# Attention scores as 64-row products of single heads, in the two halves of the array

## The chip, the cores and the metric

The kernel runs on one core of a Trainium2 chip. The metric is the device time of one execution, in microseconds. Before the change three runs took 1011.3 (median), 1008.68 and 1012.3 us. Engines are called PE (TensorE matmul; PEld is its weight load), DVE (VectorE), ACT (ScalarE), POOL (GpSimd) and SP (SyncE, which issues the DMAs). PSUM is the memory into which TensorE writes; the kernel uses it in eight buffers of one bank each.

## The reference

Pooled attention over eight batches, then two large layers (called FFN here):

```python
B, H, S, D = q.shape                      # 8, 8, 576, 64
k_p = k.reshape(B, H, Sp, 8, D).mean(axis=3)      # Sp = 72
v_p = v.reshape(B, H, Sp, 8, D).mean(axis=3)
scores = scale * np.matmul(q, k_p.transpose(0, 1, 3, 2))
scores = scores - np.max(scores, axis=-1, keepdims=True)
attn = np.exp(scores)
attn = attn / (np.sum(attn, axis=-1, keepdims=True) + 1e-09)
out = np.matmul(attn, v_p)
x = out.transpose(0, 2, 1, 3).reshape(4608, 512)
h = x @ w_in                              # 512 x 2048
g = np.maximum(0.01 * h, h)
return g @ w_out                          # 2048 x 512
```

All is F32. The kernel splits each FFN operand into a high and a low F32R part and adds three products.

## The kernel before, in words

**FFN.** The 4608 rows of x go through in chunks of 512. For a chunk and one of 16 slices of the hidden layer, `m1` adds 12 products of 512 columns into `ph` (lines 651 to 653), ACT applies the activation in place (656) and writes the high part `gh` (659), DVE writes the remainder `gl` (660). `m2` then adds 12 products into four accumulators `acc0` to `acc3` (675 to 677); it works on the slice two `m1` earlier. Each of the two yields twice, so there is a beat after every six products.

**Attention.** It is made beside the FFN. A batch's 576 queries are cut into tiles of 128 queries and one of 64, and the tiles are grouped into pieces (`PIECES`). For one tile the steps are:

- `q` (`q_unit`): four transpositions of two heads each into `qT`, so that rows 0 to 63 of a pair hold the even head's dimensions and rows 64 to 127 the odd head's (369, copied by ACT in 371).
- `sa` (`s_unit`), once for each half g of the eight heads: two products over 128 rows. Their moving operand `kT[:, p]` has 144 columns: 72 for the even head, with zeros in rows 64 to 127, and 72 for the odd head, with zeros in rows 0 to 63. So one product gives two heads' scores (394). Both go into one PSUM buffer. DVE takes the negative maximum of the four heads (402) and ACT four exps with their sums (404).
- `sb` (`norm_unit`): DVE adds 1e-9 to the four sums and takes the reciprocal (415, 416), POOL multiplies the exps into `at` (418, 422). For batch 0's tiles 2 and 3 DVE does this.
- `pu` (`p_unit`): three transpositions of `at` (443), which ACT and DVE copy into `pT` (445 to 453).
- `au` (`av_unit`), for a whole piece and half g: two head pairs, each with four products into a buffer of its own (468 to 471), copied out by ACT (479) and DVE (480) as the chunk's x.

Once for a batch, `ku` transposes the pooled keys and fills `kT` (328 to 337); `vu` fills the values and makes `v_rem` with two pairs of 32-row products (357, 360). POOL pools later batches' keys and values (229, 235); for batch 0 DVE and POOL share that.

**What sets the order.** PE runs in the order of the program (`manual_schedule`). Batch 0 goes first by a list written by hand (`FIRST`, where c is a step of converting the weights), with eight PSUM buffers in turn. From the "/" on, only the two of tag `a` serve attention, again in turn: `bank()` gives the next one, and PE waits until its last reader is done. Later batches' steps are listed by `line_up` and placed at the beats evenly over each chunk: six products or a multiple of six stand between two steps. Batch 1 runs beside the first eight slices of chunk 0, batches 2 to 7 beside the later chunks. The other engines' instructions are put in order by a scheduler from its own estimate of times, and each engine then runs its own in that order.

Tile pools: `one` has one buffer for a tag, `two` two, `three` three, `four` four. The exps' tile `e` (four heads) comes from `two`, except where `WIDE` gives batch 0's tiles room in the weights' buffers.

Of the kernel before, what the change touches and what calls it, by code (L numbers as in the profile page):

```python
# [10 lines left out]
F32 = mybir.dt.float32  # L11
# [4 lines left out]
ALU = mybir.AluOpType  # L16
# [8 lines left out]
def tile_pooled_attention_ffn(  # L25
# [38 lines left out]
    ]  # L64
    FIRST = (
# [259 lines left out]
    def place_k(b, sums, rem):  # L325
        pk = bank(b, f"pk{b}")
        for p in range(NK):
            nc.tensor.transpose(pk[:, p, :], sums[:, p, :, :].rearrange("s i d -> s (i d)"), ident)
        nc.scalar.mul(kT[0:64, :, 0, 0:MAIN], pk[0:64, :, 0:64], KSCALE)
        nc.vector.tensor_scalar_mul(kT[64:128, :, 1, 0:MAIN], pk[64:128, :, 64:128], KSCALE)  # L330
# [5 lines left out]
        nc.scalar.mul(kT[0:64, :, 0, MAIN:], prv[0:64, :, 0, :], KSCALE)  # L336
        nc.vector.tensor_scalar_mul(kT[64:128, :, 1, MAIN:], prv[64:128, :, 1, :], KSCALE)

    def place_v(b, sums, rem):
        for i in range(2):  # L340
# [38 lines left out]
    def wide_at(b, t, nm):  # L379
        return b == 0 and (nm, t) in WIDE  # L380

    def wide(b, t, g, nm, shape):
        if (nm, t) not in wides:
            wides[nm, t] = spare(*WIDE[nm, t], [P, 2, *shape], F32, f"{nm}{b}_{t}")
        return wides[nm, t][:, g]

    def s_unit(b, t, g, qT):

        n = tiles[b][t][1]
        pss = bank(b, f"pss{b}_{t}_{g}")  # L390
        sc = pss.rearrange("a p x -> a (p x)")[:, : 4 * SP]
        for i in range(2):
            p = 2 * g + i
            nc.tensor.matmul(  # L394
                sc[:n, 2 * SP * i : 2 * SP * (i + 1)], qT[:, p, :n],
                kT[:, p, :, :].rearrange("d i s -> d (i s)"), start=True, stop=True,
            )
        scv = sc.rearrange("a (h s) -> a h s", s=SP)
        e = wide(b, t, g, "e", [4, SP]) if wide_at(b, t, "e") else two.tile([P, 4, SP], F32, tag="e", name=f"e{b}_{t}_{g}")
        red = four.tile([P, 2, 4], F32, tag="red", name=f"red{b}_{t}_{g}")  # L400
        mx, sm = red[:, 0, :], red[:, 1, :]
        nc.vector.tensor_reduce(out=mx[:n], in_=scv[:n], axis=AX.X, op=ALU.max, negate=True)  # L402
        for h in range(4):
            ins = nc.scalar.activation(  # L404
                e[:n, h, :], scv[:n, h, :], AF.Exp, bias=mx[:n, h : h + 1],
                accum_out=sm[:n, h : h + 1],
            )
        if b == 0:
            anchor["act"] = ins
        return e, sm  # L410

    def norm_unit(b, t, g, e, sm):
        n = tiles[b][t][1]
        eng = nc.vector if b == 0 and t in NORM_DVE else nc.gpsimd
        nc.vector.tensor_scalar_add(sm[:n], sm[:n], 1e-9)
        nc.vector.reciprocal(sm[:n], sm[:n])  # L416
        at = wide(b, t, g, "at", [3, P]) if wide_at(b, t, "at") else three.tile([P, 3, P], F32, tag="at", name=f"at{b}_{t}_{g}")
        eng.tensor_tensor(  # L418
            at[:n, 0:2, :].rearrange("a i (h s) -> a (i h) s", h=2), e[:n, :, 0:MAIN],
            sm[:n].unsqueeze(2).broadcast_to([n, 4, MAIN]), op=ALU.mult,  # L420
        )
# [82 lines left out]
    def attention(b):  # L504
# [36 lines left out]
                    q_of[every[after]] = load_q(*every[after])  # L541
            return f

        def sa(t, g):
            def f():
                st["e", t, g] = s_unit(b, t, g, st["qT", t])
            return f

        def sb(t, g):
            def f():  # L550
                st["at", t, g] = norm_unit(b, t, g, *st["e", t, g])
            return f

        def pu(t, g):
# [7 lines left out]
        def au(j, g):  # L562
            def f():
# [3 lines left out]
        return {  # L567
            "loads": loads1 if b else loads, "lk": lk, "lv": lv, "ku": ku, "vu": vu,
            **{f"q{t}": qu(t) for t in range(len(where))},
            **{f"{n}{t}{g}": u(t, g) for n, u in (("sa", sa), ("sb", sb), ("pu", pu))  # L570
               for t in range(len(where)) for g in range(2)},
            **{f"au{j}{g}": au(j, g) for j in range(len(PIECES[b])) for g in range(2)},
        }
# [1 line left out]
    def line_up(pieces):  # L575
# [9 lines left out]
        for n, (b, j, t) in enumerate(flat):  # L585
# [5 lines left out]
                    add(b, "ku")  # L591
                add(b, f"q{t}")
            if (b, t) not in fresh:
                add(b, f"sa{t}0")
            if not first:
                add(b, f"pu{t - 1}0")
            if (b, t) not in fresh:
                add(b, f"sb{t}0")
            if nxt:
                add(nxt[0], f"q{nxt[2]}")  # L600
            add(b, f"sa{t}1")
            if n == 0 and t == 0:
                add(b, "vu")
            if last:
                if not first:
                    add(b, f"pu{t}0")
                    add(b, f"sb{t}1")
                else:
                    add(b, f"sb{t}1")
                    if nxt and nxt[0] == b:  # L610
                        add(b, f"sa{nxt[2]}0")
                        fresh[nxt[0], nxt[2]] = 1
                    add(b, f"pu{t}0")
                if nxt and nxt[0] == b and (nxt[0], nxt[2]) not in fresh:
                    add(b, f"sa{nxt[2]}0")
                    fresh[nxt[0], nxt[2]] = 1
# [222 lines left out]
```

## Time and profile before

| | us |
|---|---|
| median of three runs | 1011.3 |
| the profiled execution | 1009.92 |
| its span, first to last instruction | 1008.1 |
| PE busy | 960.3 |
| ACT busy | 427.4 |
| DVE busy | 366.3 |
| POOL busy | 177.7 |
| mean granted clock of TensorE | 0.978 |

The profile is of one execution. A row of a timeline gives the start from the span's beginning, the length, the engine, the line, the operation, out<-in, the part of the array used (rows*columns, for PE and PEld), the shape, and how many instructions are merged into the row (x4). What stands in brackets is how long the engine had been idle and what released it. Matmuls are pipelined, so the length of one (0.39 us for 512 columns) is longer than the distance to the next (0.23 us); distances between starts tell what a product costs.

### The profile page before, as it was taken

The numbers are of one execution on the slowest core, as the hardware profiler recorded it, in microseconds if no ns is written. First come the engines' busy times: TensorE is split into PE (matmuls) and PEld (weight loads), VectorE is DVE, ScalarE is ACT, GpSimd is POOL, SyncE is SP. The second block draws the span as 40 slices with busy tenths as digits, with TensorE's granted clock in tenths as the row PEclk, the third lists the DMA queues.
The fourth block names the chain that finished last, engine by engine and source line by source line (L and its number), as shares of the span: only waits on it lengthen the run. The fifth ranks groups of instructions, "written<-read, shape, count | busy, mean of one in ns | idle before, by whom it ended". The sixth has DMA issues, their size and how long they took to land.

```text
span 1008.1 us, 12812 instructions
## 1 busy us (share of the span) xinstructions
PE 960.3 (95%) x4584; PEld 785.7 (78%) x4584; DVE 366.3 (36%) x890; ACT 427.4 (42%) x1386; POOL 177.7 (18%) x292
## 2 busy tenths in 40 slices
PE   4569999999999999999999999999999999999998
PEld 4457778888887878878888788888887788888886
DVE  5998639223333222232222323232322322231111
ACT  4778657234433333434343425333434334332221
POOL 3602200501036510141013301031100001000000
PEclk8689999999999999999999999999999999999999
DMA  9954311302034301130012202020200020001001
GB/s 241 279 172 133 101 46 44 112 23 69 1 107 115 91 8 44 32 92 12 20 44 58 58 11 63 3 61 1 63 11 11 1 63 1 1 1 42 1 1 42
DMA packets 65006, 57.44 MB, mean 57 GB/s; under 512 B 39856, under 2 KB 48048, under 8 KB 64944
## 3 DMA queue, kind: packets, MB, share of 16 engines
q1 hardware_dynamic: 64944, 56.64, 19.8%
q8 instruction: 36, 0.59, 0.2%
q14 instruction: 26, 0.21, 0.1%
HBM read 46.14 MB, written 10.49 MB: 56 GB/s over the span
## 4 chain that ended last, share of the span: by engine, by line
PE 89%; DVE 4%; ACT 3%; issue 1%; DMA 1%; SPq 0%; POOL 0%; DVEq 0%; ACTq 0%; POOLq 0%
PE ph L651 13%; PE acc L675 13%; PE ph L653 13%; PE ph L652 13%; PE acc L677 13%; PE acc L676 13%; PE pss L394 4%; PE pp L443 2%; PE pq L369 2%; ACT e L404 2%; PE pa L468 1%; PE pa L469 1%; PE pa L471 1%; PE pa L470 1%; DVE w_t L187 1%
## 5 line engine op out<-in xcount | busy, mean ns | idle before, releaser
L651 PE MATMUL ph<-xh,w 128*128 128x512 f32 x576 | 236.2, 410 | 0.0
L675 PE MATMUL acc<-w,gh 128*128 128x512 f32 x576 | 234.7, 408 | 0.0
L653 PE MATMUL ph<-xh,w 128*128 128x512 f32 x576 | 227.2, 394 | 0.0
L652 PE MATMUL ph<-xl,w 128*128 128x512 f32 x576 | 227.0, 394 | 0.0
L677 PE MATMUL acc<-w,gl 128*128 128x512 f32 x576 | 225.7, 392 | 0.0
L676 PE MATMUL acc<-w,gh 128*128 128x512 f32 x576 | 225.5, 392 | 0.0
L656 ACT ACTIVATE ph<-ph 128x512 f32<-128x512 f32 x144 | 84.2, 585 | 275.6 <-PE ph L653 275.4
L660 DVE TENSOR_TENSOR gl<-ph,gh 128x512 fp32r<-128x512 f32 x144 | 99.4, 691 | 264.9 <-ACT gh L659 264.0
L418 POOL TENSOR_TENSOR at<-e,red 128x256 f32<-128x256 f32 (+1 forms) x76 | 47.3, 622 | 561.8 <-DVE red L416 428.0
L404 ACT ACTIVATE e<-pss,red 128x72 f32<-128x72 f32 (+1 forms) x320 | 98.0, 321 | 108.8 <-DVE red L402 107.3
L653 PEld LDWEIGHTS ph<-xh,w 128*128 128x128 f32 x576 | 109.3, 190 | 24.4
L677 PEld LDWEIGHTS acc<-w,gl 128*128 128x128 f32 x576 | 108.4, 188 | 24.1
L651 PEld LDWEIGHTS ph<-xh,w 128*128 128x128 f32 x576 | 109.4, 190 | 22.2 <-issue 1.4
L675 PEld LDWEIGHTS acc<-w,gh 128*128 128x128 f32 x576 | 108.4, 188 | 21.9 <-issue 1.9
L652 PEld LDWEIGHTS ph<-xl,w 128*128 128x128 f32 x576 | 109.6, 190 | 19.4
L676 PEld LDWEIGHTS acc<-w,gh 128*128 128x128 f32 x576 | 108.6, 189 | 19.2
L659 ACT CAST gh<-ph 128x512 fp32r<-128x512 f32 x144 | 85.2, 592 | 3.1
L402 DVE TENSOR_REDUCE red<-pss 128x4 f32<-128x288 f32 (+1 forms) x80 | 36.1, 454 | 99.6 <-PE pss L394 98.5
L404 ACT ACTIVATION_READ_ACCUMULATOR e<-pss,red 128x1 f32 (+1 forms) x320 | 65.8, 206 | 0.0
L394 PEld LDWEIGHTS pss<-kT,qT 128*128 128x128 f32 (+1 forms) x320 | 49.4, 192 | 14.7 <-ACT qT L371 5.0
L394 PE MATMUL pss<-kT,qT 128*128 128x144 f32 (+1 forms) x320 | 55.9, 303 | 4.2 <-ACT qT L371 4.2
L449 DVE TENSOR_TENSOR pT_lo<-pp,pT_hi 128x256 fp32r<-128x256 f32 (+1 forms) x80 | 31.6, 395 | 69.5 <-ACT pT_rem L446 68.7
(90 smaller groups left out, 857.3 us busy)
## 6 DMA issues: line engine op xcount, KB each, us to landing
out_dram<-o SPq DMA_DIRECT2D x35, 256.0 KB, 2.1
q<-in_q_dram SPq DMA_DIRECT2D x32, 256.0 KB, 4.2
w_bits<-in_moe_w_in_dram SPq DMA_DIRECT2D x16, 512.0 KB, 3.6
w_bits<-in_moe_w_out_dram SPq DMA_DIRECT2D x16, 512.0 KB, 3.4
k0raw<-in_k_dram SPq DMA_DIRECT2D x16, 256.0 KB, 3.7
k1raw<-in_k_dram SPq DMA_DIRECT2D x16, 256.0 KB, 4.4
v0raw<-in_v_dram SPq DMA_DIRECT2D x16, 256.0 KB, 4.2
v1raw<-in_v_dram SPq DMA_DIRECT2D x16, 256.0 KB, 5.4
```

Source lines behind the costliest of these rows:

```text
L394: nc.tensor.matmul(sc[:n, 2 * SP * i : 2 * SP * (i + 1)], qT[:, p, :n], kT[:, p, :, :].rearrange("d i s -> d (i s)"), start=True, stop=True,)
L404: ins = nc.scalar.activation(e[:n, h, :], scv[:n, h, :], AF.Exp, bias=mx[:n, h : h + 1], accum_out=sm[:n, h : h + 1],)
L418: eng.tensor_tensor(at[:n, 0:2, :].rearrange("a i (h s) -> a (i h) s", h=2), e[:n, :, 0:MAIN], sm[:n].unsqueeze(2).broadcast_to([n, 4, MAI ...
L651: nc.tensor.matmul(ph, w[:, 0, ks], xh[kk], start=kk == 0, stop=False)
L652: nc.tensor.matmul(ph, w[:, 0, ks], xl[kk], start=False, stop=False)
L653: nc.tensor.matmul(ph, w[:, 1, ks], xh[kk], start=False, stop=kk == NK - 1)
L656: nc.scalar.activation(ph, ph, AF.Prelu, alpha=0.01)
L659: casts.append(nc.scalar.copy(gh, ph))
L660: nc.vector.tensor_tensor(gl, ph, gh.bitcast(F32), op=ALU.subtract)
L675: nc.tensor.matmul(a, gh[:, r], hi, start=first, stop=False)
L676: nc.tensor.matmul(a, gh[:, r], lo, start=False, stop=False)
L677: nc.tensor.matmul(a, gl[:, r], hi, start=False, stop=last)
```

## The change

The scores of one tile are made in one step, `sa{t}`, in place of two. For each of the four head pairs there are two products of 64 rows and 72 columns: the even head's from rows 0 to 63 of `qT` and `kT`, the odd head's from rows 64 to 127. The even heads' scores go into one PSUM buffer and the odd heads' into another, so a step takes both buffers of tag `a`. `kT` no longer has zeros and loses a dimension; its clearing on POOL is gone. DVE takes a maximum for each of the two sides, ACT four exps for each. The tile `e` now holds all eight heads and comes from the pool with one buffer. The addition of 1e-9 and the reciprocal are made once for eight sums, and they stand at the end of `s_unit` and not in `norm_unit`. The lists `FIRST` and `line_up` name the one step where they named two, and a few neighbours change places.

The core of the diff:

```diff
-    kT = const.tile([P, NK, 2, SP], F32, name="kT")
+    kT = const.tile([P, NK, SP], F32, name="kT")
-    nc.gpsimd.memset(kT, 0.0)
...
-    def s_unit(b, t, g, qT):
+    def s_unit(b, t, qT):
         n = tiles[b][t][1]
-        pss = bank(b, f"pss{b}_{t}_{g}")
-        sc = pss.rearrange("a p x -> a (p x)")[:, : 4 * SP]
+        sides = [bank(b, f"pss{b}_{t}_{i}").rearrange("a p x -> a (p x)")[:, : 4 * SP] for i in range(2)]
+        for p in range(NK):
+            for i in range(2):
+                r = slice(64 * i, 64 * i + 64)
+                nc.tensor.matmul(
+                    sides[i][:n, SP * p : SP * (p + 1)], qT[r, p, :n], kT[r, p, :], start=True, stop=True
+                )
+        if wide_at(b, t, "e"):
+            e = wide(b, t, 0, "e", [4, SP], whole=True)
+        else:
+            e = one.tile([P, 2, 4, SP], F32, tag="e", name=f"e{b}_{t}")
+        ev = e.rearrange("a g (p i) s -> a i (g p) s", i=2)
+        red = four.tile([P, 2, 2, 4], F32, tag="red", name=f"red{b}_{t}")
+        mx, sm = (red[:, w].rearrange("a g (p i) -> a i (g p)", i=2) for w in range(2))
         for i in range(2):
-            p = 2 * g + i
-            nc.tensor.matmul(
-                sc[:n, 2 * SP * i : 2 * SP * (i + 1)], qT[:, p, :n],
-                kT[:, p, :, :].rearrange("d i s -> d (i s)"), start=True, stop=True,
-            )
...
+            scv = sides[i].rearrange("a (h s) -> a h s", s=SP)
+            nc.vector.tensor_reduce(out=mx[:n, i], in_=scv[:n], axis=AX.X, op=ALU.max, negate=True)
+            for p in range(NK):
+                ins = nc.scalar.activation(
+                    ev[:n, i, p, :], scv[:n, p, :], AF.Exp, bias=mx[:n, i, p : p + 1],
+                    accum_out=sm[:n, i, p : p + 1],
+                )
...
+        nc.vector.tensor_scalar_add(red[:n, 1], red[:n, 1], 1e-9)
+        nc.vector.reciprocal(red[:n, 1], red[:n, 1])
+        return e, red[:, 1]
...
     def norm_unit(b, t, g, e, sm):
-        nc.vector.tensor_scalar_add(sm[:n], sm[:n], 1e-9)
-        nc.vector.reciprocal(sm[:n], sm[:n])
+        e, sm = e[:, g], sm[:, g]
...
             if (b, t) not in fresh:
-                add(b, f"sa{t}0")
+                add(b, f"sa{t}")
+            if n == 0 and t == 0:
+                add(b, "vu")
...
-            add(b, f"sa{t}1")
-            if n == 0 and t == 0:
-                add(b, "vu")
```

The list by hand, before and after, up to the first value step:

```diff
-        "lk ku q0 q1 sa00 sb00 sa01 sb01 lv sa10 sb10 sa11 sb11 q2 sa20 sa21 vu pu00 pu10 c c q3 "
+        "lk ku q0 q1 sa0 sb00 sb01 lv sa1 sb10 sb11 q2 sa2 vu pu00 pu10 c c q3 "
```

Three places where the order of instructions moves follow. A row has the line, the operation, out<-in and the shape; `pss` are scores, `pa` value products, `pp` transposed probabilities, `ph` and `acc` the FFN's.

The first is PE's queue in batch 2, tile 2. Before:

```order
L394 MATMUL pss_2_0_2397<-kT,qT_2_2284 128x144 x2
L675 MATMUL acc_0_2258<-w_10_1497,gh_10_2236 128x512
L676 MATMUL acc_0_2258<-w_10_1497,gh_10_2236 128x512
L677 MATMUL acc_0_2258<-w_10_1497,gl_10_2237 128x512
L675 MATMUL acc_1_2262<-w_10_1497,gh_10_2236 128x512
L676 MATMUL acc_1_2262<-w_10_1497,gh_10_2236 128x512
L677 MATMUL acc_1_2262<-w_10_1497,gl_10_2237 128x512
L468 MATMUL pa_0_0_2413<-pT_hi,v_hi 128x256
```

After, from the last pair of the eight score products on:

```order
L397 MATMUL pss_2_0_2388<-kT,qT_2_2298 128x72
L397 MATMUL pss_2_1_2389<-kT,qT_2_2298 128x72
L653 MATMUL ph_12_2381<-xh_2_405,w_12_1594 128x512
L654 MATMUL ph_12_2381<-xl_2_409,w_12_1594 128x512
L655 MATMUL ph_12_2381<-xh_2_405,w_12_1594 128x512
L653 MATMUL ph_12_2381<-xh_3_406,w_12_1594 128x512
L654 MATMUL ph_12_2381<-xl_3_410,w_12_1594 128x512
L655 MATMUL ph_12_2381<-xh_3_406,w_12_1594 128x512
L476 MATMUL pa_0_0_2423<-pT_hi,v_hi 128x256
```

Six products stand between the scores and the value products in both; before, the scores held one of the two buffers there, now both (`pss_2_0` and `pss_2_1`).

The second is PE's queue in batch 1, tile 3. Before:

```order
L677 MATMUL acc_1_811<-w_3_620,gl_3_906 128x512
L394 MATMUL pss_3_0_1134<-kT,qT_3_1098 128x144 x2
L443 MATMUL pp_2_0_1144<-ident,at_2_0_1039 128x128 x3
L675 MATMUL acc_2_840<-w_3_620,gh_3_905 128x512
L676 MATMUL acc_2_840<-w_3_620,gh_3_905 128x512
```

After:

```order
L397 MATMUL pss_3_0_1136<-kT,qT_3_1112 128x72
L397 MATMUL pss_3_1_1137<-kT,qT_3_1112 128x72
L451 MATMUL pp_2_0_1160<-ident,at_2_0_1053 128x128 x3
L677 MATMUL acc_2_844<-w_3_622,gh_3_913 128x512
L678 MATMUL acc_2_844<-w_3_622,gh_3_913 128x512
```

The transposition follows its scores directly in both; before, it took the buffer that the scores did not hold.

The third is DVE's queue at the start, in batch 0, where `v1raw` and `vremraw` are the pooling of the values, which needs their DMA. Before:

```order
L337 TENSOR_SCALAR kT<-pkr_202 64x4x8
L402 TENSOR_REDUCE red_0_0_224<-pss_0_0_220 128x4
L229 TENSOR_TENSOR v1raw_139<-v1raw_139 128x2x256
L402 TENSOR_REDUCE red_0_1_239<-pss_0_1_235 128x4
L229 TENSOR_TENSOR vremraw_142<-vremraw_142 64x256
```

After:

```order
L337 TENSOR_SCALAR kT<-pkr_201 64x4x8
L229 TENSOR_TENSOR v1raw_138<-v1raw_138 128x2x256
L229 TENSOR_TENSOR vremraw_141<-vremraw_141 64x256
L229 TENSOR_TENSOR v1raw_138<-v1raw_138 128x2x128
L229 TENSOR_TENSOR vremraw_141<-vremraw_141 64x128
L235 TENSOR_TENSOR vsum_121<-v1raw_138 128x128
L409 TENSOR_REDUCE red_0_230<-pss_0_0_219 128x4
```

The first maximum of the scores moved behind five instructions of the values' pooling.

More of the change, by code (lines that the diff above doesn't have):

```diff
@@ L328, in place_k @@
             nc.tensor.transpose(pk[:, p, :], sums[:, p, :, :].rearrange("s i d -> s (i d)"), ident)
-        nc.scalar.mul(kT[0:64, :, 0, 0:MAIN], pk[0:64, :, 0:64], KSCALE)
-        nc.vector.tensor_scalar_mul(kT[64:128, :, 1, 0:MAIN], pk[64:128, :, 64:128], KSCALE)
+        nc.scalar.mul(kT[0:64, :, 0:MAIN], pk[0:64, :, 0:64], KSCALE)
+        nc.vector.tensor_scalar_mul(kT[64:128, :, 0:MAIN], pk[64:128, :, 64:128], KSCALE)
         pr = bank(b, f"pkr{b}")
@@ L335, in place_k @@
         prv = pr[:, 0, 0:64].rearrange("d (p i j) -> d p i j", p=NK, i=2)
-        nc.scalar.mul(kT[0:64, :, 0, MAIN:], prv[0:64, :, 0, :], KSCALE)
-        nc.vector.tensor_scalar_mul(kT[64:128, :, 1, MAIN:], prv[64:128, :, 1, :], KSCALE)
+        nc.scalar.mul(kT[0:64, :, MAIN:], prv[0:64, :, 0, :], KSCALE)
+        nc.vector.tensor_scalar_mul(kT[64:128, :, MAIN:], prv[64:128, :, 1, :], KSCALE)
     def place_v(b, sums, rem):
@@ L380, in wide_at, with wide @@
         return b == 0 and (nm, t) in WIDE
-    def wide(b, t, g, nm, shape):
+    def wide(b, t, g, nm, shape, whole=False):
         if (nm, t) not in wides:
             wides[nm, t] = spare(*WIDE[nm, t], [P, 2, *shape], F32, f"{nm}{b}_{t}")
-        return wides[nm, t][:, g]
-    def s_unit(b, t, g, qT):
+        return wides[nm, t] if whole else wides[nm, t][:, g]
+    def s_unit(b, t, qT):
         n = tiles[b][t][1]
-        pss = bank(b, f"pss{b}_{t}_{g}")
-        sc = pss.rearrange("a p x -> a (p x)")[:, : 4 * SP]
-        for i in range(2):
-            p = 2 * g + i
-            nc.tensor.matmul(
-                sc[:n, 2 * SP * i : 2 * SP * (i + 1)], qT[:, p, :n],
-                kT[:, p, :, :].rearrange("d i s -> d (i s)"), start=True, stop=True,
-            )
[L398 to L407, printed above, removed]
@@ L408, in s_unit @@
         if b == 0:
             anchor["act"] = ins
-        return e, sm
+        nc.vector.tensor_scalar_add(red[:n, 1], red[:n, 1], 1e-9)
+        nc.vector.reciprocal(red[:n, 1], red[:n, 1])
+        return e, red[:, 1]
     def norm_unit(b, t, g, e, sm):
@@ L542, in qu, with sa @@
             return f
-        def sa(t, g):
+        def sa(t):
             def f():
-                st["e", t, g] = s_unit(b, t, g, st["qT", t])
+                st["e", t] = s_unit(b, t, st["qT", t])
             return f
@@ L550, in f @@
             def f():
-                st["at", t, g] = norm_unit(b, t, g, *st["e", t, g])
+                st["at", t, g] = norm_unit(b, t, g, *st["e", t])
             return f
@@ L569, in attention @@
             **{f"q{t}": qu(t) for t in range(len(where))},
-            **{f"{n}{t}{g}": u(t, g) for n, u in (("sa", sa), ("sb", sb), ("pu", pu))
+            **{f"sa{t}": sa(t) for t in range(len(where))},
+            **{f"{n}{t}{g}": u(t, g) for n, u in (("sb", sb), ("pu", pu))
                for t in range(len(where)) for g in range(2)},
@@ L600, in line_up @@
                 add(nxt[0], f"q{nxt[2]}")
-            add(b, f"sa{t}1")
-            if n == 0 and t == 0:
-                add(b, "vu")
+            if last and not first:
+                add(b, f"pu{t}0")
+            add(b, f"sb{t}1")
             if last:
-                if not first:
+                if nxt and nxt[0] == b:
+                    add(b, f"sa{nxt[2]}")
+                    fresh[nxt[0], nxt[2]] = 1
+                if first:
                     add(b, f"pu{t}0")
[L607 to L616, printed above, removed]
                 if nxt and nxt[0] != b:
@@ L627, in line_up @@
                     add(nxt[0], "vu")
-            else:
-                add(b, f"sb{t}1")
         return out
```

4 rows, old and new, of the table FIRST are left out of this document.

## The prediction

> **What bounds the kernel now.** I read the page first: its span, busy times and the chain that ended last.
>
> ```profile
> span 1008.1 us, 12812 instructions
> PE 960.3 (95%) x4584; PEld 785.7 (78%) x4584; DVE 366.3 (36%) x890; ACT 427.4 (42%) x1386; POOL 177.7 (18%) x292
> PE 89%; DVE 4%; ACT 3%; issue 1%; DMA 1%; SPq 0%; POOL 0%; DVEq 0%; ACTq 0%; POOLq 0%
> ```
>
> TensorE carries 89% of the chain. The busy table by stage shows where that holds.
>
> ```profile
> 63.00:100.00 37.00, 32.02 (x153) 25.80 (x154) 31.81 (x75) 29.77 (x92) 5.89 (x10) 0.91 0.48 146
> 330.00:430.00 100.00, 100.00 (x483) 81.73 (x482) 29.18 (x74) 40.60 (x145) 21.11 (x35) 1.00 0.17 45
> ```
>
> The columns are PE, PEld, DVE, ACT, POOL, granted clock, DMA. Between 330 and 430 us PE is never idle, while ACT and DVE are busy 41 and 29 of 100 us: a microsecond added to or taken from TensorE's queue there goes into the time as it stands. Between 63 and 100 us PE already idles 5.0 of 37 us, so extra PE time there is partly absorbed. So I price the change by what a scores step costs in PE's queue, and by the waits that it puts there.
>
> **The step today.** The timeline of PE around one step (start, length, line; x4 because each F32 product runs as two passes):
>
> ```profile
> 603.09 0.39 PE L676 MATMUL acc<-w,gh 128*128 128x512 f32 x1
> 603.32 0.39 PE L677 MATMUL acc<-w,gl 128*128 128x512 f32 x1
> 603.54 0.65 PE L394 MATMUL pss<-kT,qT 128*128 128x144 f32 x4
> 603.94 0.49 PE L651 MATMUL ph<-xh,w 128*128 128x512 f32 x1
> 604.26 0.40 PE L652 MATMUL ph<-xl,w 128*128 128x512 f32 x1
> ```
>
> FFN products (FFN: the two big layers) start 0.23 us apart. From the last before the step to the second behind it is 0.94 us; less two intervals, the step costs 0.48 us, 0.12 for each pass of 144 columns, so 0.06 for 72. A full tile has two such steps: 0.96 us.
>
> Steps that use only 64 rows or 64 columns of the array exist already: a transposition of a 64-query tile (64*128), and that tile's scores (128*64).
>
> ```profile
> 287.24 0.39 PE L653 MATMUL ph<-xh,w 128*128 128x512 f32 x1
> 287.56 0.46 PE L369 MATMUL pq<-ident,q 64*128 64x64 f32 x4
> 287.95 0.50 PE L675 MATMUL acc<-w,gh 128*128 128x512 f32 x1
> 288.29 0.39 PE L676 MATMUL acc<-w,gh 128*128 128x512 f32 x1
> ...
> 293.82 0.39 PE L653 MATMUL ph<-xh,w 128*128 128x512 f32 x1
> 294.14 0.70 PE L394 MATMUL pss<-kT,qT 128*64 128x144 f32 x4
> 294.78 0.50 PE L675 MATMUL acc<-w,gh 128*128 128x512 f32 x1
> 295.12 0.40 PE L676 MATMUL acc<-w,gh 128*128 128x512 f32 x1
> ```
>
> By the same sum the first costs 1.05 − 0.46 = 0.59 us and the second 1.30 − 0.46 = 0.84. Their four passes account for 4 × 0.06 = 0.24 and 4 × 0.12 = 0.48. Both pay about 0.35 us more: going into another shape and back, the array runs empty (0.32 instead of 0.23 to the first product) and weight loads lie open. With the step's own first load (about 0.06 here) taken out, the toll is 0.30 us.
>
> What a weight load costs, and whether two parts of the array load at once, the v remainder's products show (32 rows each; the four belong to two different row groups). PEld rows:
>
> ```profile
> 324.19 0.29 PEld L357 LDWEIGHTS pv<-vremparts,spread 32*128 32x128 f32 x2 [0.35 <-DVE gl L660]
> ...
> 557.27 0.30 PEld L357 LDWEIGHTS pv<-vremparts,spread 32*128 32x128 f32 x4 [0.35 <-DVE xl L480]
> 557.61 0.19 PEld L651 LDWEIGHTS ph<-xh,w 128*128 128x128 f32 x1
> 557.72 0.19 PEld L652 LDWEIGHTS ph<-xl,w 128*128 128x128 f32 x1
> ```
>
> An open load of 128 columns holds the next one back by 0.11 us (557.61 to 557.72). Two loads in one group take 0.29 us, four in two groups take 0.30: the groups load side by side, although the program issues both of one group's before the other's.
>
> **The step after.** A full tile becomes 16 passes, 8 in each half of the array, of 72 columns and 128 loaded columns. If the halves run side by side and the loads set the pace, it costs 0.30 + 8 × 0.107 + 0.06 (last product) = 1.22 us against 0.96: +0.26. A 64-query tile loads 64 columns (half, about 0.055), so the product of 0.06 sets the pace: 0.30 + 0.055 + 8 × 0.06 = 0.84 against 2 × 0.84 = 1.68, −0.84. Batches 1 to 7 run in the PE-bound part, four full tiles and one of 64 each: 28 × 0.26 − 7 × 0.84 = +7.3 − 5.9 = **+1.4 us**. So halving the zero work in the products is eaten by the loads, which double in number and don't get narrower.
>
> Here a rule of the Trainium skill is to be weighed (TensorE: Matmul & The Clock Gate, Part 3, The mechanism): weights load under running products only where the row group differs. By it a half's passes would take load plus product; the trace disagrees for the whole array, where the four scores passes above come 0.12 apart with a load of 0.11 each. What it would make of the sum is the first rival.
>
> **The waits it adds.** Two PSUM buffers of tag a serve all attention steps in turn. Until now a scores step took one, and the next step had the other. Now it takes both, and the next step must wait until the first side's four exps are done, one that needs both until all eight are.
>
> ```profile
> 604.30 0.46 DVE L402 TENSOR_REDUCE red<-pss 128x4 f32<-128x288 f32 x1 [1.48 <-PE pss L394]
> 604.86 0.32 ACT L404 ACTIVATE e<-pss,red 128x72 f32<-128x72 f32 x1 [2.75 <-DVE red L402]
> ...
> 605.96 0.21 ACT L404 ACTIVATION_READ_ACCUMULATOR e<-pss,red 128x1 f32 x1
> ```
>
> The products' last columns stream until about 604.03 (the first FFN product's start of 603.94 plus its extra 0.09); the four exps end at 606.17, 2.14 us later, and four more end at 3.36 (their own 1.22 on top; the second maximum hides under the first exps). After the step the array needs 0.2 us to come back, then each FFN product 0.23. With six of them in between, the next step comes at 1.58 us and waits 0.6 for the first buffer; twelve put it at 2.96, behind it. The order has, in batches 1 to 7, eleven places with six products or fewer; with twelve and more I count nothing. Five are probability transpositions (0.6 each, 3.0). Three are value products that need both buffers: 0.6, then four passes of 0.12, then 0.7 for the second, 1.3 each, 3.9. One of these waits already:
>
> ```profile
> 254.19 0.28 PE L471 MATMUL pa<-pT_rem,v_rem 128*128 128x256 f32 x1
> 254.99 0.39 PE L468 MATMUL pa<-pT_hi,v_hi 128*128 128x256 f32 x1 [0.52 <-ACT e L404]
> ...
> 234.82 0.40 PE L357 MATMUL pv<-vremparts,spread 32*128 32x64 f32 x2
> 235.74 0.41 PE L357 MATMUL pv<-vremparts,spread 32*128 32x64 f32 x2 [0.52 <-DVE v_rem L360]
> ```
>
> That is 0.80 instead of 0.12 apart, so 3.9 − 0.7 = 3.2. Two are the v remainder's pairs: 1.8 each for both buffers, of which 0.8 is waited today (0.92 between the pairs less 0.1), so 2.0. And in batch 1 a transposition follows its scores with no product between: 2.0. Together 10.2 us. 5.5 of it (1.0, 1.3, two of 0.6, 2.0) falls into batch 1, where PE idles already; I take half of that away: **+7.4 us**. Bounds: 3 (all of batch 1 and half the rest absorbed) and 13 (an FFN activation of ACT slipping between the exps at some of the twelve-product places).
>
> Waits can cost the clock as well. After the wait of 1.6 us at 324 the granted clock fell:
>
> ```profile
> 324.00:328.00 4.00, 2.81 (x11) 2.13 (x10) 2.43 (x6) 0.33 (x2) 2.15 (x4) 0.81 0.46 139
> 328.00:332.00 4.00, 4.00 (x16) 3.38 (x16) 0.78 (x3) 1.32 (x8) 2.47 (x3) 0.77 0.53 155
> ```
>
> That loses 4 × 0.19 + 4 × 0.23 = 1.7 us. Waits of 0.7 and 0.8 us did not do it; new ones of 1.3 to 2 us may. One such event: **+1.7** (bounds 0 and 5).
>
> **The start.** DVE's order puts batch 0's v sums ahead of the first maximum. Today:
>
> ```profile
> 14.34 0.46 DVE L402 TENSOR_REDUCE red<-pss 128x4 f32<-128x288 f32 x1 [2.40 <-PE pss L394]
> 15.00 0.74 DVE L229 TENSOR_TENSOR v1raw<-v1raw 128x512 f32<-128x512 f32 x1 [0.20 <-DMA v1raw<-in_v_dram]
> 16.03 0.40 DVE L229 TENSOR_TENSOR vremraw<-vremraw 64x256 f32<-64x256 f32 x1
> 16.36 0.41 DVE L229 TENSOR_TENSOR v1raw<-v1raw 128x256 f32<-128x256 f32 x1
> 17.50 0.27 DVE L229 TENSOR_TENSOR vremraw<-vremraw 64x128 f32<-64x128 f32 x1
> 17.70 0.28 DVE L235 TENSOR_TENSOR vsum<-v1raw 128x128 f32<-128x128 f32 x1
> ```
>
> The maximum ran at 14.34 and the sums wait for their DMA until 15.00; their five spans (2.1 us) now come first, so the exps start up to 2.8 us later. DVE does the same sums either way, does fewer additions and reciprocals, and kT's clearing on POOL is gone, so part returns: **+1.2** (bounds −1 and +2.8).
>
> Nothing for the rest: the merged additions and reciprocals (DVE is idle most of the time; what queues behind them, the FFN remainder gl, is needed two FFN blocks of 24 products later); the single e buffer (the next scores stand eighteen FFN products or more later, outside batch 1; without that cover ACT would wait for POOL's normalisation); POOL's sums and SP's loads change places by a row or two.
>
> **Sum.** 1.4 + 7.4 + 1.7 + 1.2 = +11.7. The profiled execution took 1009.9 us (span 1008.1); the runs' median is 1011.3. So 1021.6 for a like execution and 1023.0 beside the median; I take 1022.
>
> **Rivals.**
> Loads not under products within a half: full tiles 0.30 + 8 × 0.168 + 0.06 = 1.70, 64-query tiles 0.30 + 8 × 0.116 = 1.23: 28 × 0.74 − 7 × 0.45 = +17.6 instead of +1.4, 1038 us. Against it speaks the spacing of 0.12 above; chance 0.08.
> The change doesn't do what it says, and the halves run one after the other: 0.30 + 16 × 0.107 + 0.06 = 2.07 and 0.30 + 0.055 + 16 × 0.06 = 1.32: 28 × 1.11 − 7 × 0.36 = +28.6, 1049 us. For it: no F32 pass in two halves stands in the trace; against it the four loads in 0.30 us. Chance 0.10.
> The waits are absorbed: idle time that PE has anyway in batch 1 takes them all, and the other places pay half. Then 1.4 + 2.4 leaves 1014. Chance 0.17.
> The other side, faster: a load of half the rows takes half the time. The transpositions' loads of 64 rows and 128 columns did come 0.06 apart, in the transposing mode. Then a full tile is 0.30 + 0.055 + 8 × 0.06 = 0.84: 28 × −0.12 − 5.9 = −9.3. With all waits at 10.2 that only breaks even; with half of them absorbed and no lost clock it gives −4 to −9, about 1003. It decides as soon as a pass takes under 0.06 us and the waits under 9 us. Chance 0.10. The Trainium skill's rule (TensorEngine Tiling, Theoretical Speedup) that contraction over 64 rows or fewer gains up to a factor of two stands on this side: two steps of 0.48 would become one of 0.48, with neither toll nor load. The 0.59 us of the 64-row step above speaks against it.
>
> **How the numbers follow.** Forecast 0.55, its own range 1012 to 1033 from the bounds above. A measurement of this kernel can tell about 0.5% from no change, 1006 to 1016 us. Slower: 0.47 of the forecast, both slow rivals: 0.65. Same: 0.08 of the forecast and 0.15 of the absorbed case: 0.23. Faster: 0.12. The range 1006 to 1040 leaves out the case of serial halves and the faster one.
>
> **What would show it.** Right: scores steps of 1.2 us (full) and 0.84 (64 queries), loads of two halves at the same time; PE waits for the exps at the eleven places, ACT as releaser; the first exp at about 17 us. Wrong: loads in the halves 0.06 or 0.2 apart per pair, PE never waiting for exps, or more lost in clock than in waits.

## The result, and the profile after

The changed kernel takes 1032.52 us (median of 4 runs, 1031.38 to 1034.93), the kernel before 1010.09 beside it: ratio 1.0222, 95% interval 1.0204 to 1.0241. Its profiled execution took 1032.99 us, 23.1 more than that of before; span and shares from its page:

```profile
span 1031.2 us, 13315 instructions
PE 964.5 (94%) x4904; PEld 781.2 (76%) x4904; DVE 353.4 (34%) x810; ACT 425.1 (41%) x1386; POOL 176.1 (17%) x291
PE 77%; ACT 6%; DVE 5%; DMA 5%; POOL 3%; issue 2%; SPq 1%; POOLq 0%; DVEq 0%; ACTq 0%
```

TensorE is busy 4 us longer in a span that is 23 us longer, and its share of the chain falls from 89% to 77%: the time went into waiting. The busy table by stage says the same (PE, PEld, DVE, ACT, POOL, granted clock, DMA):

```profile
63.00:100.00 37.00, 27.28 (x129) 20.56 (x130) 31.03 (x64) 28.42 (x87) 4.79 (x8) 0.82 0.55 165
330.00:430.00 100.00, 96.96 (x511) 78.07 (x510) 28.85 (x70) 40.38 (x148) 29.41 (x47) 1.00 0.22 57
```

Between 330 and 430 us, where PE never idled before, it now idles 3 us; between 63 and 100 us it is 9.7 us instead of 5.0.

**Where along the program.** Both kernels issue the same 3456 FFN products in the same order on TensorE, so the start of the n-th is a clock that can be compared. The first, and the 193rd (batch 1 is done by then), in the timelines of the kernel before and of the changed one:

```profile
51.94 0.50 PE L651 MATMUL ph<-xh,w 128*128 128x512 f32 x1
139.38 0.39 PE L651 MATMUL ph<-xh,w 128*128 128x512 f32 x1
```
```profile
60.23 0.50 PE L653 MATMUL ph<-xh,w 128*128 128x512 f32 x1
154.56 0.39 PE L653 MATMUL ph<-xh,w 128*128 128x512 f32 x1
```

Start of the n-th FFN product in each profiled execution (e1 to e12 are the experiments below; that of e9 and that of e12 were the slowest of their six runs, some 4 us above the median):

| n | before | after | e1 | e3 | e6 | e9 | e10 | e12 |
|---|---|---|---|---|---|---|---|---|
| 1 | 51.94 | 60.23 | 55.47 | 59.41 | 55.74 | 57.09 | 59.68 | 56.77 |
| 193 | 139.38 | 154.56 | 146.69 | 156.76 | 150.82 | 151.16 | 153.62 | 151.62 |
| 1249 | 419.54 | 437.57 | 428.67 | 436.98 | 438.03 | 435.13 | 437.57 | 434.04 |
| 3456 | 1002.98 | 1025.95 | 1009.56 | 1019.08 | 1025.81 | 1018.58 | 1022.05 | 1015.81 |

So of 23.0 us, 8.3 are there before the first FFN product, 6.9 come in batch 1, 7.8 later. Between the first and the last FFN product PE's idle times of 0.15 us and more add up to 17.6 us before and 29.8 after, 12.2 more. The time lost there to a lower clock (length times what the granted clock lacks of 1) is 8.5 us in both.

**The step itself.** Timeline of PE around a full tile's scores and around a 64-query tile's, changed kernel:

```profile
253.12 0.39 PE L655 MATMUL ph<-xh,w 128*128 128x512 f32 x1
253.43 1.12 PE L397 MATMUL pss<-kT,qT 64*128 64x72 f32 x16
254.48 0.50 PE L653 MATMUL ph<-xh,w 128*128 128x512 f32 x1
254.82 0.39 PE L654 MATMUL ph<-xl,w 128*128 128x512 f32 x1
...
536.77 0.39 PE L655 MATMUL ph<-xh,w 128*128 128x512 f32 x1
537.09 0.72 PE L397 MATMUL pss<-kT,qT 64*64 64x72 f32 x16
537.74 0.50 PE L677 MATMUL acc<-w,gh 128*128 128x512 f32 x1
538.08 0.40 PE L678 MATMUL acc<-w,gh 128*128 128x512 f32 x1
```

By the prediction's sum: 1.70 − 0.46 = 1.24 us and 1.31 − 0.46 = 0.85. Against two old steps (0.96 and 1.68) that is 28 × 0.28 − 7 × 0.83 = +2.0 us in batches 1 to 7.

**The start.** VectorE's first maximum ran at 14.34 before. Now five rows of v sums stand ahead of it, and the first of them waits for its DMA until 16.73:

```profile
16.73 0.69 DVE L229 TENSOR_TENSOR v1raw<-v1raw 128x512 f32<-128x512 f32 x1 [5.04 <-DMA v1raw<-in_v_dram]
...
18.82 0.46 DVE L409 TENSOR_REDUCE red<-pss 128x4 f32<-128x288 f32 x1
```

ScalarE too has other work ahead, both halves of v_hi:

```profile
18.89 0.85 ACT L342 ACTIVATE v_hi<-vsum 64x256 fp32r<-64x256 f32 x2 [5.21 <-DVE vsum L235]
19.77 0.32 ACT L411 ACTIVATE e<-pss,red 128x72 f32<-128x72 f32 x1
```

The first exp starts at 19.77 us, 4.9 later than before.

**A wait behind a scores step**, at 654 us (batch 5, tile 4: value products with six FFN products behind the scores). PE, ACT and DVE:

```profile
652.58 0.40 PE L679 MATMUL acc<-w,gl 128*128 128x512 f32 x1
654.13 0.38 PE L476 MATMUL pa<-pT_hi,v_hi 128*128 128x256 f32 x1 [1.15 <-ACT e L411]
...
655.34 0.38 PE L476 MATMUL pa<-pT_hi,v_hi 128*128 128x256 f32 x1 [0.47 <-ACT e L411]
...
652.76 0.32 ACT L411 ACTIVATE e<-pss,red 128x72 f32<-128x72 f32 x1 [1.18 <-DVE red L409]
...
651.61 0.69 DVE L662 TENSOR_TENSOR gl<-ph,gh 128x512 fp32r<-128x512 f32 x1 [4.68 <-ACT gh L661]
652.22 0.81 DVE L409 TENSOR_REDUCE red<-pss 128x4 f32<-128x288 f32 x2
```

PE waits for exps, as predicted. But read on: the exps waited for the maximum, and the maximum stood in VectorE's queue behind gl, a row of the FFN, which had itself waited 4.68 us for ScalarE's gh. The last pass of the scores had started at 651.1 us, 1.1 before the maximum; where nothing stands ahead of it, the maximum follows after 0.3 (median of e9's steps below).

### The profile page after: what moved, and what is told of

It is laid out like the page before. It is cut to its first block, busy times and chain, and to the rows that moved or that the text cites. A ratio compares the mean times of both kernels' runs of the same rounds, so it can differ in the third digit from the quotient of the medians.

```text
span 1031.2 us, 13315 instructions
## 1 busy us (share of the span) xinstructions
PE 964.5 (94%) x4904; PEld 781.2 (76%) x4904; DVE 353.4 (34%) x810; ACT 425.1 (41%) x1386; POOL 176.1 (17%) x291
## 4 chain that ended last, share of the span: by engine, by line
PE 77%; ACT 6%; DVE 5%; DMA 5%; POOL 3%; issue 2%; SPq 1%; POOLq 0%; DVEq 0%; ACTq 0%
PE ph L653 12%; PE acc L677 11%; PE ph L655 11%; PE ph L654 11%; PE acc L679 11%; PE acc L678 11%; ACT e L411 4%; PE pss L397 2%; PE pp L451 2%; DMA vremraw<-in_v_dram 2%; PE pq L369 1%; DVE w_t L190 1%; SPq L241 1%; DMA out_dram<-o 1%; PE pa L477 1%
## 5 line engine op out<-in xcount | busy, mean ns | idle before, releaser
L411 ACT ACTIVATION_READ_ACCUMULATOR e<-pss,red 128x1 f32 (+1 forms) x320 | 68.3, 214 | 0.0
L451 PE MATMUL pp<-ident,at 128*128 128x128 f32 (+1 forms) x240 | 41.4, 285 | 19.8 <-POOL at L426 5.6
L451 PEld LDWEIGHTS pp<-ident,at 128*128 128x128 f32 (+1 forms) x240 | 30.0, 149 | 37.0 <-issue 16.0
L397 PEld LDWEIGHTS pss<-kT,qT 64*128 64x128 f32 (+1 forms) x640 | 39.4, 192 | 19.8 <-issue 10.5
```

Source lines behind the costliest of these rows:

```text
L397: nc.tensor.matmul(sides[i][:n, SP * p : SP * (p + 1)], qT[r, p, :n], kT[r, p, :], start=True, stop=True)
L411: ins = nc.scalar.activation(ev[:n, i, p, :], scv[:n, p, :], AF.Exp, bias=mx[:n, i, p : p + 1], accum_out=sm[:n, i, p : p + 1],)
L451: nc.tensor.transpose(pp[:, i, :n], at[:n, i, :], ident[:n, :n])
```

## The experiments

**e1: the old products in the merged step.** Everything of the change but the 64-row form.

```diff
...
-                    sides[i][:n, SP * p : SP * (p + 1)], qT[r, p, :n], kT[r, p, :], start=True, stop=True
...
+                sides[g][:n, 2 * SP * i : 2 * SP * (i + 1)], qT[:, p, :n],
+                kT[:, p, :, :].rearrange("d i s -> d (i s)"), start=True, stop=True,
...
```

> The changed kernel with the old 128-row products of 144 columns against zero-padded keys in the merged step: one step, two buffers, the same order and DVE work (and one red buffer fewer, for space). The theory (the 64-row products cost nothing on balance, the start and the two-buffer waits cost it all) expects the time of the changed kernel, 1029 to 1034 us, with full-tile steps of about 0.96 us and 64-query steps of about 1.3 to 1.4 (one shape toll instead of two). The rival (the tolls and loads of the 64-row products are what costs) expects the time before, 1010 to 1014 us.

Measured 1015.09 us, ratio to before 1.0037 (1.0023 to 1.0051). The theory fell: merging costs 4 us, the 64-row form the other 17. Its step price is no reason for 17; PE around a full and a 64-query tile:

```profile
638.69 0.39 PE L656 MATMUL ph<-xh,w 128*128 128x512 f32 x1
638.92 1.14 PE L397 MATMUL pss<-kT,qT 128*128 128x144 f32 x8
639.80 0.49 PE L678 MATMUL acc<-w,gh 128*128 128x512 f32 x1
640.13 0.39 PE L679 MATMUL acc<-w,gh 128*128 128x512 f32 x1
...
303.48 0.39 PE L656 MATMUL ph<-xh,w 128*128 128x512 f32 x1
303.80 1.19 PE L397 MATMUL pss<-kT,qT 128*64 128x144 f32 x8
304.92 0.50 PE L678 MATMUL acc<-w,gh 128*128 128x512 f32 x1
305.26 0.40 PE L679 MATMUL acc<-w,gh 128*128 128x512 f32 x1
```

0.98 and 1.32 us (one toll instead of two), so the 64-row form is dearer by 28 × 0.26 − 7 × 0.47 = 4.0 us. 13 more were to be found.

**e2: batch 0 the old way.**

```diff
-        "lk ku q0 q1 sa0 sb00 sb01 lv sa1 sb10 sb11 q2 sa2 vu pu00 pu10 c c q3 "
+        "lk ku q0 q1 sa00 sb00 sa01 sb01 lv sa10 sb10 sa11 sb11 q2 sa20 sa21 vu pu00 pu10 c c q3 "
...
+            **{f"{n}{t}{g}": u(t, g) for n, u in (("sa", sa_old), ("sb", sb), ("pu", pu))
...
```

> The changed kernel with batch 0 done the old way: two steps a tile, 128-row products, its old order of units, additions and reciprocals with the normalisation; batches 1 to 7 as changed. The theory (about 8 us of the 22 arise at the start, where DVE's queue delays the first maximum and tile 2's normalisation) expects the first FFN product back within 1 us of its place before, and 1022 to 1026 us. The rival (the start's delay is absorbed by batch 1, where TensorE idles anyway, so removing it gives nothing) expects 1030 to 1033 us.

Measured 1031.94 us, 1.0205 (1.0180 to 1.0231): the rival. The first FFN product starts at 53.90, 6.3 us earlier than after, the 193rd at 149.88 (4.7 earlier), the 1249th at 437.01 (0.6). What is won at the start is lost again by then.

**e3: room behind the scores.**

```diff
...
-                    while done < min(len(us), len(us) * beat // (beats - 4)):
+                    while done < min(len(us), len(us) * beat // (beats - 4)) and beat >= free:
                         us[done]()
+                        if n >= 2 and us[done].__qualname__.split(".")[-3] == "sa":
+                            free = beat + 3
```

> The changed kernel with at least 18 FFN products between a scores step and the next attention step, in batches 2 to 7 (the later steps move back by a place or two; batch 1 as it is). The theory (waits for the two buffers cost 6 to 8 us there) expects no wait of over 0.5 us on exps behind a scores step after 200 us and 1024 to 1027 us. The rival (the loss behind batch 1 is the products themselves or the clock) expects 1031 to 1034 us.

Measured 1026.14 us, 1.0149 (1.0127 to 1.0170): as expected. From the 193rd FFN product to the last it takes 862.3 us, the kernel before 863.6: batches 2 to 7 cost nothing any more.

**e4: both sides through one half** (the odd heads' scores are computed from the even heads' rows).

```diff
-                r = slice(64 * i, 64 * i + 64)
+                r = slice(0, 64)
```

> The changed kernel with the products of both sides on rows 0 to 63: the odd heads' scores are computed from the even heads' queries and keys, so 16 passes of 72 columns go through one half of the array. If the halves run side by side, a full-tile step becomes 0.30 + 16 x 0.107 + 0.06 = 2.07 us instead of 1.25 and a 64-query step 1.32 instead of 0.85: 28 x 0.82 + 7 x 0.47 = +26 us, 1055 to 1062 us. If they run one after the other already, nothing changes: 1030 to 1035 us.

One execution: 1051.92 us. PE around a full tile:

```profile
256.31 0.39 PE L655 MATMUL ph<-xh,w 128*128 128x512 f32 x1
256.63 2.00 PE L397 MATMUL pss<-kT,qT 64*128 64x72 f32 x16
258.56 0.50 PE L653 MATMUL ph<-xh,w 128*128 128x512 f32 x1
258.90 0.39 PE L654 MATMUL ph<-xl,w 128*128 128x512 f32 x1
```

2.13 us instead of 1.24 (2.07 was expected; the whole is 3 us under the range): the halves do run side by side, and the change does what it says. Eight further passes in a half add 0.89 us, 0.111 each; with 0.06 of product and 0.107 of load one after the other it would be 0.167. That speaks against the Trainium skill's rule (TensorE: Matmul & The Clock Gate, Part 3, The mechanism) that a load runs under products only of another row group: here it runs under products of the same rows. The same section also lets a load that goes to a background weight buffer be pulled ahead; no run here shows whether these loads do.

**e5: the first bank complete last** (e1's order of products turned round).

```diff
-        for p in range(NK):
+        for p in (2, 3, 0, 1):
```

> The merged step with the old 128-row products, but the second bank's two products issued first, so that the bank whose maxima and exps come first is complete only at the step's end, 0.5 us later in the same queue. TensorE's own work is that of the first experiment. The theory (what the 64-row form adds to the waits is that both banks become complete only with the last passes, so the maxima start later behind the step) expects 0.3 to 0.5 us more at each of the places with six FFN products behind the scores, 2 to 5 us in all: 1017 to 1020 us. The rival (the 64-row passes cost in another way) expects the first experiment's time, 1013 to 1016 us.

Measured 1012.93 us, 1.0020 (1.0010 to 1.0029), the rival's time. But the edit did not do what it was meant to: the first maximum starts 0.69 us after the step's first pass in e1 (237.25 after 236.56) and in e5 (233.79 after 233.10), so VectorE again takes the bank that fills first, and TensorE, VectorE, ScalarE and GpSimd run the same lists of work in both. The theory stays untested by this run. In the changed kernel with e1's order (e9, below) the first maximum starts 1.15 us after the first pass (median of 35 steps), in e1 0.76. What e1 and e5 do show is how far two runs of the same work can lie apart: 2.2 us.

**e6: the maxima first, at the start.**

```diff
-        "lk ku q0 q1 sa0 sb00 sb01 lv sa1 sb10 sb11 q2 sa2 vu pu00 pu10 c c q3 "
+        "lk ku q0 q1 sa0 sb00 sb01 sa1 lv sb10 sb11 q2 sa2 vu pu00 pu10 c c q3 "
...
+            with nullcontext() if b else tc.issue_after(anchor["top"].ins):
...
```

> The changed kernel with one edit at the start: VectorE's part of batch 0's v sums is queued behind the maxima of tiles 0 and 1, as the kernel before has it for the most part. The theory (that order costs 4 to 5 of the 8 us by which the first FFN product is late, the merged steps the rest) expects the first exp at 14.7 to 15.5 us, the first FFN product 4 to 5 us earlier than in the changed kernel, and 1026 to 1029 us. The rival (batch 1, where TensorE waits anyway, absorbs it) expects the first FFN product earlier but 1031 to 1034 us.

Measured 1032.88 us, 1.0212 (1.0192 to 1.0231): the rival again. The first exp starts at 15.76 and the first FFN product 4.5 us earlier, but the gain is gone by the 1249th product (table above). It went at about 338 to 363 us, where PE waits for batch 3's v remainder. ScalarE, VectorE and PE there, e6:

```profile
354.69 0.26 ACT L351 ACTIVATE vremparts<-vremsum 64x64 fp32r<-64x64 f32 x1 [5.12 <-POOL vremsum L235]
...
354.98 2.83 DVE L352 SCALAR_TENSOR_TENSOR vremparts<-vremsum,vremparts 64x64 fp32r<-64x64 f32 x1 [5.28 <-ACT vremparts L351]
...
358.47 0.50 PE L658 MATMUL ph<-xh,w 128*128 128x512 f32 x1 [2.22 <-DVE gl L667]
```

The remainder's parts wait for GpSimd, GpSimd for a DMA. The FFN's cast gh stands behind them on ScalarE and gl on VectorE, whose row on the parts takes 2.83 us: TensorE waits 2.22 us for gl. The changed kernel has the same order there and waits too, but there the row takes 0.42 us:

```profile
358.08 0.26 ACT L348 ACTIVATE vremparts<-vremsum 64x64 fp32r<-64x64 f32 x1 [6.77 <-POOL vremsum L235]
...
358.37 0.42 DVE L349 SCALAR_TENSOR_TENSOR vremparts<-vremsum,vremparts 64x64 fp32r<-64x64 f32 x1 [6.60 <-ACT vremparts L348]
...
359.58 0.50 PE L653 MATMUL ph<-xh,w 128*128 128x512 f32 x1 [1.59 <-DVE gl L662]
```

So the DMA is not what took the gain: the parts still come 3.4 us earlier in e6 (354.69 against 358.08), the product behind gl only 1.1 us (358.47 against 359.58). And in e6 this wait and one before it were each followed by a stretch at half clock (busy table, columns as above); the changed kernel's clock is 1.00 in both stretches (the first is shown). e6, and then the changed kernel:

```profile
342.00:346.00 4.00, 4.00 (x24) 2.89 (x22) 0.00 (x0) 0.00 (x0) 0.25 (x1) 0.60 0.78 204
...
359.00:363.00 4.00, 4.00 (x11) 2.83 (x10) 0.01 (x1) 0.00 (x0) 2.65 (x3) 0.59 0.13 20
```
```profile
342.00:346.00 4.00, 2.62 (x12) 2.21 (x13) 2.02 (x5) 0.00 (x0) 2.93 (x5) 1.00 0.10 23
```

That is 4 × 0.40 + 4 × 0.41 = 3.2 us of the 4.2 by which e6 falls back between the 193rd and the 1249th product (from 3.7 ahead to 0.5 behind).

**A new theory.** Only TensorE's order is written out in this kernel; a scheduler sorts VectorE's and ScalarE's queues by when it believes each row's inputs to be ready. From e1 to the changed kernel 109 of VectorE's 810 places and 59 of ScalarE's 1065 change, though both issue the same work. VectorE's queue at the place of 654 us, from e1 (−) to after (+):

```
 TENSOR_TENSOR gl_4<-ph_4,gh_4 128x512
+TENSOR_TENSOR gl_5<-ph_5,gh_5 128x512
 TENSOR_REDUCE red_4<-pss_4_0 128x4
 TENSOR_REDUCE red_4<-pss_4_1 128x4
-TENSOR_TENSOR gl_5<-ph_5,gh_5 128x512
```

In eight places gl slips ahead of a pair of maxima; elsewhere it is a result copy that waits for a DMA, the remainder's parts, rows that convert weights (batch 1), or the v sums (the start). All would fit a scheduler that takes the 16 passes for slow. So the order itself was tried, as a table, both ways.

**e9: the changed kernel in e1's order; e10: e1 in the changed kernel's order; e11: e9 with VectorE's queue alone.**

```diff
...
+    for engine, table in ((nc.vector.engine, ORDER_DVE), (nc.scalar.engine, ORDER_ACTIVATION)):
+        mine = [i for i in traced if i.engine == engine]
+        want = [int(x) for x in table.split()]
...
+        for x, y in zip(want, want[1:]):
+            tc.add_manual_dep(
+                mine[y], mine[x].name,
...
```

> The changed kernel, 64-row products and all, with VectorE's and ScalarE's queues put in the order that the scheduler gave the first experiment (a table; 109 of VectorE's 810 places and 59 of ScalarE's 1065 change, nothing else does). New theory: the 64-row form costs its 17 us over the first experiment because the scheduler, which sorts these two queues by when it believes inputs are ready, believes the 16 passes slow and puts other work, some of it waiting for a DMA or GpSimd, ahead of the maxima and of the FFN casts. It expects 1012 to 1018 us. The rival (the passes themselves) expects 1029 to 1034 us.

> The reverse: the first experiment (old 128-row products in the merged step) with VectorE's and ScalarE's queues in the order of the changed kernel. The same theory expects it slower by most of the 17 us, 1026 to 1032 us; the rival expects the first experiment's time, 1012 to 1017 us.

> The changed kernel with VectorE's queue alone in the order of the first experiment; ScalarE's is the scheduler's own, which then differs from the first experiment's in 27 places. If VectorE's order carries the cost (v sums, result copies and FFN remainders ahead of maxima), 1013 to 1020 us; if ScalarE's does (casts ahead of others, the v remainder's parts ahead of an FFN cast), 1025 us or more.

e9: 1021.26 us, 1.0106 (1.0086 to 1.0126). e10: 1029.64, 1.0184 (1.0169 to 1.0200). e11: 1022.04, 1.0107 (1.0088 to 1.0126). The order alone makes e1 14.6 us slower, and takes 11.3 of its 22 us from the changed kernel. With VectorE's queue alone the time is the same; but ScalarE's queue then falls into e1's order too, except in 27 places, so the two are not quite separated. e9 and e11 came 2 to 3 us over what was expected, since that left out the 4 us by which the 64-row steps are dearer: 1015.1 + 4.0 = 1019.1; 2 us stay unexplained, no more than e1 and e5 differ by.

Between the first and the last FFN product of each profiled execution (us):

| | before | e1 | e9 | e10 | after |
|---|---|---|---|---|---|
| PE idle | 17.6 | 20.9 | 21.0 | 30.2 | 29.8 |
| lost to the clock | 8.5 | 8.2 | 15.0 | 6.8 | 8.5 |

The order costs 9 us of waiting there, with either form of the products, and a later start (60.23 against 57.09, 59.68 against 55.47). In these executions it is not the clock: e10 and the changed kernel lose 6.8 and 8.5 us to it, e1 8.2. The place of 654 us again, in e1 and then in e10, whose products are the same:

```profile
641.61 0.39 PE L477 MATMUL pa<-pT_hi,v_hi 128*128 128x256 f32 x1 [0.15 <-ACT e L412]
...
639.68 0.88 DVE L410 TENSOR_REDUCE red<-pss 128x4 f32<-128x288 f32 x2 [4.01 <-PE pss L397]
640.47 0.68 DVE L663 TENSOR_TENSOR gl<-ph,gh 128x512 fp32r<-128x512 f32 x1
```
```profile
652.00 0.38 PE L548 MATMUL pa<-pT_hi,v_hi 128*128 128x256 f32 x1 [1.42 <-ACT e L483]
...
649.48 0.69 DVE L734 TENSOR_TENSOR gl<-ph,gh 128x512 fp32r<-128x512 f32 x1 [4.68 <-ACT gh L733]
650.09 0.81 DVE L481 TENSOR_REDUCE red<-pss 128x4 f32<-128x288 f32 x2
```

Maximum before gl: the wait is 0.15 us. gl before the maximum: 1.42. In e9, with the 64-row products and the maximum before gl, it is 0.43.

**e12: order and room together** (the edit of e3, and as a table the order that e1 has when it is given that room).

> The changed kernel with both repairs: 18 FFN products of room behind each scores step of batches 2 to 7, and VectorE's and ScalarE's queues in the order that the scheduler gives the first experiment when it has that room too. If order and room each take away waits that the other leaves (the waits for the two buffers behind batch 1 still cost some 4 us in the repaired order), 1016 to 1019 us; what is then left over the kernel before lies in the start and batch 1. If the order alone had taken away all that the room can, 1020 to 1023 us. Neither theory expects it to reach the kernel before.

Measured 1018.61 us, 1.0066 (1.0044 to 1.0087): as expected. In its profiled execution all that is left over the kernel before is there by the 193rd FFN product (151.62 against 139.38 in the table, 12.2 of 12.8 us).

**e7 and e8: the toll, put to use in the kernel before.** e7 pads the scores of 64-query tiles to the whole array's shape, e8 their transpositions as well.

```diff
+        if b and n < P:
+            nc.vector.memset(qT[:, :, n:], 0.0)
...
+        m = P if b else n
...
-                sc[:n, 2 * SP * i : 2 * SP * (i + 1)], qT[:, p, :n],
+                sc[:m, 2 * SP * i : 2 * SP * (i + 1)], qT[:, p, :m],
...
```

> The kernel before, with one edit: in batches 1 to 7 the scores of a 64-query tile load all 128 columns of its transposed queries (the other 64 are set to zero on VectorE), so that the array is not put into another shape. The theory (a step in another shape pays a toll of 0.30 to 0.35 us) expects 14 steps of 0.48 instead of 0.84: -5.0 us, 1005 to 1007 us. The rival (the 64-query step is slow for another reason, its rows or its loads) expects 1009 to 1012 us.

> The same for the 64-query tiles' transpositions as well: queries and probabilities are padded with 64 rows of zeros (set on VectorE), so that these steps too keep the whole array's shape. The theory expects a further 7 x 0.14 (queries) and 14 x 0.19 (probabilities), -8.6 us against the kernel before: 1001 to 1004 us. The rival (the settings to zero stand in VectorE's queue and their waits take the gain back) expects 1005 us or more.

e7: 1006.53 us, 0.9959 (0.9944 to 0.9974). e8: 1003.69, 0.9923 (0.9900 to 0.9947). Both as expected. PE around a 64-query tile's scores in e7:

```profile
293.98 0.39 PE L656 MATMUL ph<-xh,w 128*128 128x512 f32 x1
294.21 0.65 PE L397 MATMUL pss<-kT,qT 128*128 128x144 f32 x4
294.60 0.49 PE L678 MATMUL acc<-w,gh 128*128 128x512 f32 x1
294.93 0.40 PE L679 MATMUL acc<-w,gh 128*128 128x512 f32 x1
```

0.95 − 0.46 = 0.49 us instead of 0.84, for twice the columns: the toll comes with the change of shape and goes with it. e8 is the fastest version of this study, ahead of both kernels.

## Why the sign and the range held, and where the prediction's steps failed

The time was forecast at 1022 us, with a range to 1040, and is 1032.5: the change costs 22 us, and the sum had 11.7. That the kernel gets slower was right, and so was the kind of loss, TensorE waiting for exps behind a scores step. But half of the loss came from the new order of VectorE's and ScalarE's queues, of which the prediction priced only a part, at the start. That the time still lies in the range is in part luck: the forecast's own bounds end at 1033, half a microsecond above it, and the range reached 1040 for a slow rival that did not come true. In the profiled executions the 23.0 us are 8.3 at the start, 2.0 in the scores steps and 12.2 of idle time, where 1.2, 1.4 and 7.4 had been put; the clock, with 1.7 in the sum, added nothing. The steps:

- **The products, +1.4 us: right.** 1.24 and 0.85 us against 1.22 and 0.84, +2.0 in all; halves side by side (e4), toll by shape (e7). Both rivals on the array itself, serial halves and loads not under products, are out, and so is the faster one: a pass of a half takes 0.111 us, not under 0.06.
- **The waits, +7.4: mechanism and places right, the size partly by luck.** At the eleven places that were counted PE waits 11.2 us in all for the exps (4.0 of it at five transpositions where the profile names no releaser), against about 2 us of waits there before; 10.2 more had been put. Room behind the scores of batches 2 to 7 (e3) takes away 6.4 us, where 4.7 of waits and 1.7 of clock had been put. But part of this is the order again: in e9 the same places wait 9.4 us, and there the room brings only 2.7 us (e9 to e12). The step that was wrong is that the maxima follow their products at once, so that four exps end 2.14 us after the last columns. In the changed kernel this holds for 21 of the 35 steps of batches 1 to 7 (2.1 to 2.2 us after the start of the last pass); in 14, other rows stand ahead of the maxima and it is 2.5 to 5.6 us. So the pair of value products at 654 us waits 1.15 + 0.47 us where e1 waits 0.15 + 0.46.
- **"Nothing for the rest": wrong, and the largest miss.** The prediction looked at VectorE's new order at the start and nowhere else. The rows that changed place along the whole program cost 11.3 us (e9) to 14.6 (e10), more than any term of the sum. (These figures hold the order's share of the start and of the waits too, so they cannot be added to the other terms.)
- **The start, +1.2: wrong in size, and misjudged in worth.** The first FFN product is 8.3 us late, not 1.2. The five v sums on VectorE were counted; not counted were that their DMA landed at 16.73 instead of 15.00, and ScalarE's v_hi ahead of the exps. In e10, with this order and the sums from 14.80 on, the first exp starts at 17.64, about the 17 that was forecast; in the changed kernel at 19.77. Why the DMA lands later there is open. Undoing the start alone, however, brings nothing (e2, e6): the gain is gone by the 1249th product, in e6 by the long row on the v remainder and the clock, in e2 by longer waits for exps (3.9 us against 1.1 between the 193rd and the 1249th) and one stretch at half clock.
- **One half-clock event, +1.7: it came, but it was not an addition.** Behind the wait at 654 us the clock fell, a loss of 4 × 0.42 = 1.7 us:

```profile
656.00:660.00 4.00, 4.00 (x12) 3.12 (x12) 0.44 (x2) 0.38 (x1) 0.87 (x2) 0.58 0.00 0
```

The kernel before loses the same 1.7 us at 324 to 332 us, the very event that gave the size, and the changed kernel loses nothing behind the waits of that place (1.00 from 342 to 346 us, and from 330 to 430). The net is nothing.

- **Half of batch 1's waits absorbed: not seen.** Batch 1 added 6.9 us although PE idled there before; only 2.8 had been left to it. PE's waits for exps, with those without a named releaser, rose there by 3.9 us; others came on top in that stretch, above all for GpSimd's normalisation (2.9 to 5.3 us).

What stays open: how the 7 us of e12 divide between merged steps at the start and in batch 1, and the 2 us of e9 that the steps do not explain; that both banks now fill together, so that the first maximum starts later, is a candidate that no run isolates. That the scheduler misprices the 16 passes is argued from the rows that moved; shown is that the order, whatever made it, costs what it does.

## What to carry to other kernels

Where a scheduler orders the queues that you did not write out, a new form of an instruction can change those queues along the whole program: compare every engine's order before and after, and put a price on each row that now stands ahead of the one TensorE waits for. A step on a part of the array pays to go there and back, so a short tile padded with zeros to the whole shape can be cheaper than its exact size. A gain at the start is not yet a gain at the end: 4.5 and 6.3 us (e6, e2) were gone by the 1249th of 3456 products, so a start has to be priced by the time of the whole.

## What the runs showed of the hardware

- Two 64-row halves with F32 products of 72 columns run side by side although the program alternates between them; a half takes a pass every 0.111 us, the pace of its 128-column loads, so halving the rows gains nothing (1.24 us for 16 half passes, 0.98 for 8 whole ones of 144 columns).
- A step in another array shape costs 0.35 us more than the same step in the whole shape (0.84 against 0.49), whether or not it does less work.
- Waits of the same length do not always cost the clock: after 1.15 and 0.47 us at 654 us the granted clock fell to 0.58, after 1.42 and 0.47 us at the same place in e10 it stayed at 1.00:

```profile
656.00:660.00 4.00, 4.00 (x21) 3.27 (x20) 1.00 (x3) 1.71 (x4) 0.97 (x2) 1.00 0.00 0
```

- VectorE's 64 x 64 operation on the remainder's parts of batch 3 took 2.83 us in e6, 2.84 in e2, 2.87 in e9 and e12, and 0.42 in the changed kernel. In e6 GpSimd worked without a break beside it and paused at 357.73 us, just before it ended at 357.81; but GpSimd worked beside the short one too. What held it was not tested.
